# Routing tokens to experts by scattered token numbers, the gate as a column of the row, and logits by pairs of chunks

## The chip, the cores and the metric

The kernel runs on one core of one Trainium2 chip. The metric is the device time of one execution in microseconds (us). Three executions of the kernel before took 446.55, 448.6 and 443.81 us; their median is 446.55.

## What is computed

The reference is a gated linear attention whose result goes through a mixture of experts. Four batches, eight heads, 768 steps, head size 48; `x` is then 3072 tokens by 384.

```
state = alpha[:, :, t, :, None] * state + k[:, :, t] outer v[:, :, t]
y[:, :, t] = q[:, :, t] @ state
x = y.transpose(0, 2, 1, 3).reshape(3072, 384)
logits = x @ w_gate + modality_bias[modality_id]          # 8 experts
e_idx = argmax(logits)
gate = exp(0) / (sum(exp(logits - max)) + 1e-9)
out[token] = gate * (relu(x[token] @ w1[e_idx]) @ w2[e_idx])
```

w1[e] is 384 x 1024 and w2[e] 1024 x 384, all float32. Each token goes to one expert, so the tokens of an expert have to be brought together before its two products.

## The kernel before

**Attention.** The 3072 tokens are 24 chunks of 128, six to a batch. A loop over `s` runs the steps of several chunks side by side: loads of q, k, v, alpha on SP, `decay` (two scans on DVE, L238 and L245), `scale` (L261, L264), `scores` (L273 on PE, a copy on ACT L277, and the causal mask L278, an affine select on POOL, twice per chunk), and three steps later `combine`: the state's update (matmuls L305 into the PSUM tile "kv", DVE L308), the output matmuls L318 and L320, and the copy `yt` (L322). From `yt` the chunk's logits are made: L341 multiplies it with the gate weights into "kv", ACT copies that (`lts`), L347 sums the four head pairs by a matmul with `sel8` into "kv" again, and DVE adds the bias (L348). "kv" has one buffer. `rows` transposes yt (L329) and writes 128 rows of x to the DRAM table `xd`.

**Routing.** After chunks 5, 11, 15, 17, 21 and 23 a route group (table GROUPS) takes the logits of the 6, 6, 4, 2, 4 and 2 chunks since the last group: the maximum, the first expert that reaches it (one small DVE operation per chunk, L396), one-hots, the rank of each token among its expert's tokens by matmuls with a triangle (L400 to L406), and then per chunk on DVE the token's own rank (L408), the number of full 128s in it (L418) and a plane `OL`, 128 x 128, that holds the token's number at its rank (L424). Slots of 256 tokens of one expert are the units of the experts' work. The table of which token stands where in a slot is a sum of matmuls of those planes with one-hots of the slots: for slots 0 and 1 early, after chunks 15 and 17 (`route_early`, L508), for all others in `route_end` once chunk 23 is done, where counts of tokens become runs, keys (L549, L553), the schedule `meta` (L554) and 24 matmuls (L566, marked "table"). `places` makes `idx` (for gathers) and `odx` (for the output) of it. The gates are made apart (`gates`), written to DRAM as a column `gd` and gathered by the same indices (`gather_gates`, L611).

**Experts.** Twelve full slots, then conditional ones: at slot i, inside `If(ns > i)`, either a full slot or a half one of 128 tokens. In this run there is one half slot, 12. For each slot SP loads the weights (4 transfers of 768 KB, two sets of buffers), POOL gathers rows (`xg`, L606, two of 128 rows, three buffers) and gates; `prep` transposes the rows on PE (L758); `split` makes high and low parts of weights on ACT and DVE (L767, L769), and the products are three matmuls each (L788 to L790, L809 to L811; half slot L838 and L850 to L852). The output rows are scaled by the gate (L813, half slot L854) and scattered to DRAM on POOL (L815, L856). `prep(i + 1)` is called at the end of slot i.

**What sets the order.** Each engine runs its instructions in the order in which a scheduler put them before the launch; a waiting instruction holds everything behind it on its engine. `issue_after` keeps a few matmuls behind marks: the first layer of slot 0 is cut into steps by the table STEPS, and layer 2 of slot 0 comes after the mark "table".

## Time and profile before

| what | before |
|---|---|
| three executions | 446.55, 448.6, 443.81 us |
| the profiled execution, its span | 449.16 us, 447.4 us |
| mean granted clock of PE | 0.969 |
| busy: PE, PEld, DVE, ACT, POOL | 406.1, 369.5, 280.3, 238.3, 135.6 us |
| last copy of yt (attention done) | 190.0 us |
| schedule of the slots known (`meta`) | 206.7 us |
| one full slot | 17.6 us |
| last output scatter | 429.0 us |

The busy rows say how long each engine ran at all. A window row gives for a stretch of time the busy time of each engine, with the number of instructions, the granted clock and the DMA engines' share. A row of a group ends in the idle time that its engine had ahead of it and in what ended that idle time. PEld is the loading of weights into PE, which runs beside the matmuls. All times of single instructions are from the span's start.

### The profile page before, as it was taken

The numbers are of one execution on the slowest core, as the hardware profiler recorded it, in microseconds if no ns is written. First come the engines' busy times: TensorE is split into PE (matmuls) and PEld (weight loads), VectorE is DVE, ScalarE is ACT, GpSimd is POOL, SyncE is SP. The second block draws the span as 40 slices with busy tenths as digits, with TensorE's granted clock in tenths as the row PEclk, the third lists the DMA queues.
The fourth block names the chain that finished last, engine by engine and source line by source line (L and its number), as shares of the span: only waits on it lengthen the run. The fifth ranks groups of instructions, "written<-read, shape, count | busy, mean of one in ns | idle before, by whom it ended". The sixth has DMA issues, their size and how long they took to land. (4 is left out here: it accounts for less than half of the span.)

```text
span 447.4 us, 10022 instructions
## 1 busy us (share of the span) xinstructions
PE 406.1 (91%) x3784; PEld 369.5 (83%) x3784; DVE 280.3 (63%) x659; ACT 238.3 (53%) x455; POOL 135.6 (30%) x183
## 2 busy tenths in 40 slices
PE   3999998999999899887999999999999999999620
PEld 3878887888788678665999999999999999999620
DVE  7877679687959793476964766575575675430400
ACT  3476766666575544373655757556565565332310
POOL 9321212111121523200727524343353332110500
PEclk9999999999999899996999999999999999999985
DMA  7999776477556766103997785585586765730200
GB/s 148 202 195 207 145 170 134 99 163 170 114 108 145 268 219 237 38 19 95 379 387 236 279 285 165 203 307 192 193 258 214 232 205 170 262 109 20 58 14 1
DMA packets 134685, 78.81 MB, mean 176 GB/s; under 512 B 103905, under 2 KB 121374, under 8 KB 134616
## 3 DMA queue, kind: packets, MB, share of 16 engines
q1 hardware_dynamic: 130328, 67.72, 54.3%
q0 software_dynamic: 4288, 10.24, 6.3%
q8 instruction: 35, 0.57, 0.5%
q14 instruction: 34, 0.28, 0.2%
HBM read 68.49 MB, written 9.65 MB: 175 GB/s over the span
## 5 line engine op out<-in xcount | busy, mean ns | idle before, releaser
L769 DVE TENSOR_TENSOR w2L<-w2r,w2H 128x768 fp32r<-128x768 f32 x52 | 49.3, 956 | 51.8 <-ACT w2H L767 50.5
L788 PE MATMUL tr<-xH,w1H 128*128 128x256 f32 x264 | 75.8, 287 | 2.4 <-DVE hL L794 2.3
L789 PE MATMUL tr<-xL,w1H 128*128 128x256 f32 x264 | 74.8, 283 | 0.0
L790 PE MATMUL tr<-xH,w1L 128*128 128x256 f32 x264 | 74.6, 283 | 0.0
L278 POOL TENSOR_SCALAR_AFFINE_SELECT scT<-scT 128x512 f32<-128x512 f32 x48 | 30.8, 664 | 121.5 <-ACT scT L277 121.5
L809 PE MATMUL sc<-w2H,hH 128*128 128x384 f32 x192 | 64.4, 337 | 0.0
L810 PE MATMUL sc<-w2L,hH 128*128 128x384 f32 x192 | 64.0, 335 | 0.0
L811 PE MATMUL sc<-w2H,hL 128*128 128x384 f32 x192 | 62.6, 335 | 0.0
L767 ACT CAST w2H<-w2r 128x768 fp32r<-128x768 f32 x52 | 42.7, 833 | 35.4 <-PE sc L811 30.7
L815 POOL DMA_INDIRECT out_dram<-os,odx x24 | 25.9, 1078 | 103.0 <-ACT os L813 70.7
L769 DVE TENSOR_TENSOR w1L<-w1r,w1H 128x768 fp32r<-128x768 f32 x44 | 41.8, 957 | 22.2 <-ACT w1H L767 17.7
L788 PEld LDWEIGHTS tr<-xH,w1H 128*128 128x128 f32 x264 | 50.6, 192 | 3.0 <-DVE hL L794 2.5
L767 ACT CAST w1H<-w1r 128x768 fp32r<-128x768 f32 x44 | 36.3, 834 | 31.0 <-PE tr L789 18.5
L789 PEld LDWEIGHTS tr<-xL,w1H 128*128 128x128 f32 x264 | 50.7, 192 | 0.0
L790 PEld LDWEIGHTS tr<-xH,w1L 128*128 128x128 f32 x264 | 50.4, 191 | 0.0
L606 POOL DMA_INDIRECT xg<-xd,idx x28 | 35.0, 1251 | 43.8 <-DVE vals L475 29.4
L320 PE MATMUL y<-scT,vt 128*64 128x128 f32 x384 | 44.4, 279 | 0.0
L318 PE MATMUL y<-qh,UB 128*64 128x128 f32 x320 | 41.0, 282 | 0.4 <-ACT UB L299 0.4
L794 DVE SCALAR_TENSOR_TENSOR hL<-tr,hH 128x512 fp32r<-128x512 f32 x48 | 32.9, 685 | 13.0 <-ACT hH L792 13.0
L611 POOL DMA_INDIRECT gg<-gd,idx x28 | 31.9, 1138 | 18.9 <-DMA gd<-gs 9.1
L792 ACT ACTIVATE hH<-tr 128x512 fp32r<-128x512 f32 x48 | 28.5, 593 | 16.1 <-PE tr L790 8.7
L809 PEld LDWEIGHTS sc<-w2H,hH 128*128 128x128 f32 x192 | 36.3, 189 | 0.0
(220 smaller groups left out, 810.8 us busy)
## 6 DMA issues: line engine op xcount, KB each, us to landing
w1r<-in_moe_w_dram SPq DMA_DIRECT2D x28, 768.0 KB
w2r<-in_moe_w_dram SPq DMA_DIRECT2D x28, 768.0 KB
nat_a<-in_alpha_dram SPq DMA_DIRECT2D x24, 192.0 KB
nat_k<-in_k_dram SPq DMA_DIRECT2D x24, 192.0 KB
nat_q<-in_q_dram SPq DMA_DIRECT2D x24, 192.0 KB
vt<-in_v_dram SPq DMA_DIRECT2D x24, 192.0 KB
xd<-xs SPq DMA_DIRECT2D x24, 192.0 KB
xg<-xd,idx POOLq DMA_INDIRECT x28, 6.6
```

What stands on the lines that cost most here:

```text
L318: pe.matmul(y[r, j], U[:, j, g], qh[:, j], start=True, stop=False)
L320: pe.matmul(y[r, j], vt[:, 2 * j + g], sc[g][:, j], start=(c == 0), stop=True)
L606: pool.indirect_dma_start(xg[i % NX][:, u], None, xd[0:rows], ix, bounds_check=rows - 1, oob_is_err=False)
L767: act.copy(hi, src)
L769: vec.tensor_tensor(lw, src, hi.bitcast(F32), op=ALU.subtract)
L788: pe.matmul(hp[:, z], wH[:, d, fs], xH[:, d], start=(d == 0), stop=False)
L789: pe.matmul(hp[:, z], wH[:, d, fs], xL[:, d], start=False, stop=False)
L790: pe.matmul(hp[:, z], wL[:, d, fs], xH[:, d], start=False, stop=(d == ND - 1))
L794: vec.scalar_tensor_tensor(hL, hp, 0.0, hH.bitcast(F32), op0=ALU.max, op1=ALU.subtract)
L809: pe.matmul(op, hH[:, z, us], wH[:, z], start=(f == 0), stop=False)
L810: pe.matmul(op, hH[:, z, us], wL[:, z], start=False, stop=False)
L811: pe.matmul(op, hL[:, z, us], wH[:, z], start=False, stop=(f == NF - 1))
```

## The change

The table of places is not summed by matmuls any more but written by scatters. Each expert has 3072 places in a DRAM table `tab`, filled with an empty mark at the start. A route group computes for each token its place, expert base plus rank, as one number `dst` (the base is carried in the running counts `ohs`, which start at 24 x 128 x e), and POOL scatters the chunk's 128 token numbers there, one transfer per chunk (L425, 24 in all). A slot is a run of 256 places: SP loads the place at which it begins (`begin`, L544), then the 256 numbers (`ids`, L545), and POOL gathers the rows by them (L548); the output scatter uses the same `ids`. The planes OL, the one-hots OH, `places` and the marks "key0" and "table" go; layer 2 of slot 0 stands behind the mark "key".

The small operations of a route group are done for all its chunks at once (L397 to L422), the exponentials for the gate among them. The gate becomes column 384 of the row: `xs` holds the rows of a whole group and goes out in one write after the group's reciprocal (L431, 6 writes, before 24), and a gather brings row and gate together. `gates`, `gd` and `gather_gates` go.

Logits are made for two chunks at a time: L341 has 256 columns, two transposes (L346) take the place of two L347, and one DVE reduction (L347 of the new kernel) sums the four head pairs; the bias is added by group.

In the conditional slots `prep(i)` stands at the start of slot i's own `If` instead of at the end of slot i - 1, so that prep(13) is run only where a slot 13 exists.

The core of the diff:

```diff
-STEPS = (("key", 21), ("key0", 20), ("count", 9), ("rank", 8), ("logits", 6), ("logitst", 4))
+STEPS = (("key", 18), ("count", 9), ("rank", 8), ("logits", 6), ("logitst", 4))
...
-    xd = dr.tile([N + 1, DM], F32, name="xd")
-    gd = dr.tile([N + 1, 1], F32, name="gd")
+    xd = dr.tile([N, W], F32, name="xd")
+
+    tab = dr.tile([E * N, 1], I32, name="tab")
...
-    xg = [cp.tile([P, 2, DM], F32, name=f"xg{i}") for i in range(NX)]
-    gg = [cp.tile([P, 2], F32, name=f"gg{i}") for i in range(NX)]
+    xg = [cp.tile([P, 2, W], F32, name=f"xg{i}") for i in range(NX)]
+
+    NI = 4
+    ids = [cp.tile([P, 2], I32, name=f"ids{i}") for i in range(NI)]
...
+    pool.iota(ti, [[P, NU]], base=0, channel_multiplier=1)
+    none = ac.tile([P, E * NU], I32, name="none")
+    pool.memset(none, EMPTY)
+    sp.dma_start(tab.rearrange("(p x) o -> p (x o)", p=P), none)
+    for t in xg:
+        pool.memset(t, 0.0)
...
-        yt = sb.tile([P, NP, P], F32, name="yt")
-        mark["yt"] = act.copy(yt, y)
-        st[i, "y"] = yt
-
-    def rows(i):
+        yt = sb.tile([P, 2, NP, P], F32, name="yt") if i % 2 == 0 else st[i - 1, "yt"]
+        mark["yt"] = act.copy(yt[:, i % 2], y)
+        st[i, "yt"], st[i, "y"] = yt, yt[:, i % 2]
...
-        sp.dma_start(xd[row(i) : row(i) + P, :], xs)
...
     def logits(i, after=None):
 
-        lt = ps.tile([P, P], F32, name="kv")
+        lt = ps.tile([P, 2, P], F32, name="kv")
         with issue_after(after):
             for j in range(NP):
                 mark["logitst"] = pe.matmul(
-                    lt[32 * j : 32 * j + 32], wgp[:, j], st[i, "y"][:, j], start=True, stop=True
+                    lt[32 * j : 32 * j + 32], wgp[:, j], st[i, "yt"][:, :, j], start=True, stop=True
                 )
-        ls = sb.tile([P, P], F32, name="lts")
+        ls = sb.tile([P, 2, P], F32, name="lts")
         mark["xc"] = act.copy(ls, lt)
-        lp = ps.tile([P, E], F32, name="kv")
-        mark["logits"] = pe.matmul(lp, ls, sel8, start=True, stop=True)
-        vec.tensor_tensor(L[:, i], lp, bt[:, i], op=ALU.add)
+        lp = ps.tile([P, 2, P], F32, name="kv")
+        for c in range(2):
+            mark["logits"] = pe.transpose(lp[:, c], ls[:, c], ident)
+        vec.tensor_reduce(
+            L[:, i - 1 : i + 1], lp.rearrange("p c (j e) -> p c e j", e=32)[:, :, :E], axis=AX.X, op=ALU.add
+        )
...
+        vec.tensor_tensor(L[:, s], L[:, s], bt[:, s], op=ALU.add)
         vec.tensor_reduce(mx[:, s], L[:, s], axis=AX.X, op=ALU.max)
-        for t in range(t0, t1):
-            vec.scalar_tensor_tensor(eq[:, t], L[:, t], mx[:, t : t + 1], rev, op0=ALU.is_equal, op1=ALU.mult)
+        vec.tensor_tensor(ls[:, s], L[:, s], wide(mx), op=ALU.subtract)
+        act.activation(ex[:, s], ls[:, s], AF.Exp)
+        vec.scalar_tensor_tensor(
+            eq[:, s], ls[:, s], 0.0, rev.unsqueeze(1).broadcast_to(sh), op0=ALU.is_equal, op1=ALU.mult
+        )
         vec.tensor_reduce(m2[:, s], eq[:, s], axis=AX.X, op=ALU.max)
-        vec.tensor_tensor(oh[:, s], eq[:, s], m2[:, s].unsqueeze(2).broadcast_to(sh), op=ALU.is_equal)
+        vec.tensor_tensor(oh[:, s], eq[:, s], wide(m2), op=ALU.is_equal)
...
-        for t in range(t0, t1):
-            vec.scalar_tensor_tensor(
-                rj, rp[:, t - t0], 1.0, oh[:, t], op0=ALU.mult, op1=ALU.mult, accum_out=r1[:, t : t + 1]
-            )
...
+        vec.tensor_reduce(sm[:, s], ex[:, s], axis=AX.X, op=ALU.add)
+        vec.tensor_scalar(sm[:, s], sm[:, s], 1e-9, None, op0=ALU.add)
+        vec.reciprocal(xs[:, :n, DM], sm[:, s])
+        vec.tensor_tensor(rk[:, s], rp, oh[:, s], op=ALU.mult)
+        with nc.allow_low_precision("whole numbers"):
+            vec.tensor_reduce(dst[:, s], rk[:, s], axis=AX.X, op=ALU.add)
...
         for t in range(t0, t1):
-            vec.scalar_tensor_tensor(
-                hj, thr, r1[:, t : t + 1], onh, op0=ALU.is_le, op1=ALU.mult, accum_out=hr[:, t : t + 1]
+            d = pool.indirect_dma_start(
+                tab, IOA(dst[:, t : t + 1], 0), ti[:, t : t + 1], None, bounds_check=E * N - 1, oob_is_err=False
             )
-        vec.scalar_tensor_tensor(hi[:, s], m2[:, s], -float(NU), hr[:, s], op0=ALU.mult, op1=ALU.add)
-        vec.scalar_tensor_tensor(lo[:, s], hr[:, s], -float(P), r1[:, s], op0=ALU.mult, op1=ALU.add)
-        for t in range(t0, t1):
-            vec.tensor_scalar(OL[:, t], ioh, lo[:, t : t + 1], tok[:, t : t + 1], op0=ALU.is_equal, op1=ALU.mult)
...
+        sp.dma_start(xd[t0 * P : t1 * P].rearrange("(t p) w -> p t w", p=P), xs[:, :n])
...
-        vec.tensor_scalar(key0, iof[:, :2], off, None, op0=ALU.add)
-        vec.tensor_tensor(
-            OHE[:, :n],
-            key0.unsqueeze(1).broadcast_to([P, n, 2]),
-            hi[:, :n].unsqueeze(2).broadcast_to([P, n, 2]),
-            op=ALU.is_equal,
-        )
-        tp = ps.tile([P, 2], F32, name="rt")
-        for t in range(n):
-            pe.matmul(tp, OL[:, t], OHE[:, t], start=(t == 0), stop=(t == n - 1))
-        places(tp, slice(2 * s, 2 * s + 2))
+            vec.tensor_scalar(off, base, -float(N), None, op0=ALU.mult)
+        vec.tensor_scalar(begin[:, s : s + 1], off[0:1], float(E * N), None, op0=ALU.add)
...
-        kp = ps.tile([P, 2, NH], F32, name="rt")
-        mark["key0"] = pe.matmul(kp[:, 0, :nh], ones[:nh], diag[:nh, 0, :nh], start=True, stop=True)
-        vec.tensor_copy(key[:, :nh], kp[:, 0, :nh])
-        vec.scalar_tensor_tensor(rg, beg[:, :NG], sz, dE, op0=ALU.is_le, op1=ALU.mult, accum_out=kc[:, 1:2])
-        vec.tensor_scalar(diag[:, 1], ident[:, :NH], kc[:, 1:2], None, op0=ALU.mult)
-        mark["key"] = pe.matmul(kp[:, 1, :nh], ones[:nh], diag[:nh, 1, :nh], start=True, stop=True)
-        vec.tensor_copy(meta[:, na:NS], kp[0:1, 1, 0:nh:2])
-        tp = ps.tile([P, nh], F32, name="rt")
-        for g in range(3):
-            n = NU // 3
-            z = slice(g * n, (g + 1) * n)
-            vec.tensor_tensor(
-                OH[:, z, :nh],
-                key[:, :nh].unsqueeze(1).broadcast_to([P, n, nh]),
-                hi[:, z].unsqueeze(2).broadcast_to([P, n, nh]),
-                op=ALU.is_equal,
...
+        vec.tensor_tensor(rg, dC, rm.unsqueeze(1).broadcast_to([P, 2, NG]), op=ALU.mult)
+        vec.tensor_reduce(kc, rg, axis=AX.X, op=ALU.add)
+        kp = ps.tile([1, 2, ns], F32, name="rt")
+        for u in range(2):
+            mark["key"] = pe.matmul(kp[:, u], kc[:ns, u : u + 1], ident[:ns, :ns], start=True, stop=True)
+        vec.tensor_copy(meta[:, na:NS], kp[:, 1])
+        vec.tensor_tensor(begin[:, na:], ior[:, :ns], kp[:, 0], op=ALU.add)
...
             )
-            for t in range(g * n, (g + 1) * n):
-                mark["table"] = pe.matmul(tp, OL[:, t], OH[:, t, :nh], start=(t == 0), stop=(t == NU - 1))
...
-    def gates(t0, t1):
-        z = slice(t0, t1)
-        sh = [P, t1 - t0, E]
-        vec.tensor_tensor(ls[:, z], L[:, z], mx[:, z].unsqueeze(2).broadcast_to(sh), op=ALU.subtract)
...
-    def gather(i, rows=N + 1):
+    def gather(i, rows=N):
+        r = sp.value_load(begin[0:1, i : i + 1], min_val=0, max_val=E * N - T)
+        sp.dma_start(ids[i % NI], tab[bass.ds(r, T)].rearrange("(u p) o -> p (u o)", p=P))
         for u in range(2):
-            ix = IOA(idx[:, 2 * i + u : 2 * i + u + 1], 0)
+            ix = IOA(ids[i % NI][:, u : u + 1], 0)
             pool.indirect_dma_start(xg[i % NX][:, u], None, xd[0:rows], ix, bounds_check=rows - 1, oob_is_err=False)
-
-    def gather_gates(i, rows=N + 1):
...
+            for _, t0, t1 in GROUPS:
+                if t0 <= s - 3 < t1:
+                    if t0 == s - 3:
+                        xsg = sb.tile([P, max(b - a for _, a, b in GROUPS), W], F32, name="xs")
+                    rows(s - 3, xsg[:, s - 3 - t0])
+            if (s - 3) % 2:
+                logits(s - 3, ("step", ND - 1) if s - 3 == NU - 1 else None)
             for after, t0, t1 in GROUPS:
                 if after == s - 3:
-                    route_group(t0, t1)
+                    route_group(t0, t1, xsg)
                     if t1 in EARLY:
                         e = EARLY.index(t1)
                         route_early(e)
                         weights(e, e)
-                        gather(e, row(t1))
-                        if e == NA - 1:
-                            gates(0, t1)
-                            for e in range(NA):
-                                gather_gates(e, row(t1))
+                        gather(e, t1 * P)
...
-            g = gg[i % NX]
+            g = xg[i % NX][:, :, DM]
...
-                with issue_after("table" if ahead and i == 0 else None):
+                with issue_after("key" if ahead and i == 0 else None):
...
-                ix = IOA(odx[:, 2 * i + u : 2 * i + u + 1], 0)
+                ix = IOA(ids[i % NI][:, u : u + 1], 0)
...
                 with tc.If(ns > i):
+                    if i > NS0:
+                        prep(i)
                     with tc.If(nfl > i) as full:
                         ahead_of(i + 1)
                         act.copy(XH[i % 2], xf)
                         vec.tensor_tensor(XL[i % 2], xf, XH[i % 2].bitcast(F32), op=ALU.subtract)
                         slot(i)
-                        if i + 1 < NS:
-                            prep(i + 1)
                     with full.Else():
                         ahead_of(i + 1)
                         half(i)
-                        if i + 1 < NS:
-                            prep(i + 1)
                     tail(i + 1)
```

**The order on POOL.** These rows are POOL's program from the first chunks to the first slots: the affine selects of the scores (two per chunk), gathers of rows (`xg`), of gates (`gg`), and with the change scatters of token numbers (`tab<-ti,dst`). Before:

```order
L278 AFFINE_SELECT scT<-scT 128x512 x40
L606 DMA xg_116<-xd,idx 128x384 x2
L278 AFFINE_SELECT scT<-scT 128x512 x4
L606 DMA xg_117<-xd,idx 128x384 x2
L278 AFFINE_SELECT scT<-scT 128x512 x2
L611 DMA gg_119<-gd,idx 128x1 x2
L611 DMA gg_120<-gd,idx 128x1 x2
L278 AFFINE_SELECT scT<-scT 128x512 x2
L606 DMA xg_118<-xd,idx 128x384 x2
```

The same stretch of the changed kernel:

```order
L277 AFFINE_SELECT scT<-scT 128x512 x18
L425 DMA tab<-ti,dst 24576x1 x6
L277 AFFINE_SELECT scT<-scT 128x512 x12
L425 DMA tab<-ti,dst 24576x1 x6
L277 AFFINE_SELECT scT<-scT 128x512 x8
L425 DMA tab<-ti,dst 24576x1 x4
L277 AFFINE_SELECT scT<-scT 128x512 x4
L548 DMA xg_116<-xd,ids_119 128x385 x2
L425 DMA tab<-ti,dst 24576x1 x2
L277 AFFINE_SELECT scT<-scT 128x512 x3
L548 DMA xg_117<-xd,ids_120 128x385 x2
```

The first six scatters stand between the selects of chunk 8 and those of chunk 9; the gathers of gates are gone.

**The order on DVE at the transition**, behind the last route group: `hL` are the low parts of slot 0's hidden layer, of which there are four, `w1L`, `w2L` the splits of weights, `kc` and `meta` the end of the schedule. Before:

```order
L794 SCALAR_TENSOR_TENSOR hL<-tr,hH 128x512
L547 SCALAR_TENSOR_TENSOR diag<-ident,kc,dz 128x38
L551 SCALAR_TENSOR_TENSOR rg,kc<-beg,sz,dE 128x16
L552 TENSOR_SCALAR diag<-ident,kc 128x38
L550 CAST key<-rt 128x34
L559 TENSOR_TENSOR OH<-key,hi 128x8x34 x3
L554 CAST meta<-rt 1x17
L794 SCALAR_TENSOR_TENSOR hL<-tr,hH 128x512
```

With the change:

```order
L723 SCALAR_TENSOR_TENSOR hL<-tr,hH 128x512
L520 TENSOR_REDUCE kc<-rg 128x2
L698 TENSOR_TENSOR w2L<-w2r_113,w2H 128x768
L723 SCALAR_TENSOR_TENSOR hL<-tr,hH 128x512
L524 CAST meta<-rt 1x17
L525 TENSOR_TENSOR begin<-ior,rt 1x17
L698 TENSOR_TENSOR w2L<-w2r_113,w2H 128x768 x3
L690 TENSOR_TENSOR xL_2860<-kv,xH_2858 128x512
L690 TENSOR_TENSOR xL_2860<-y,xH_2858 128x256
L698 TENSOR_TENSOR w1L<-w1r_114,w1H 128x768 x4
L698 TENSOR_TENSOR w2L<-w2r_115,w2H 128x768 x2
L723 SCALAR_TENSOR_TENSOR hL<-tr,hH 128x512 x2
```

Before, the fourth hL of slot 0 follows `meta` at once; now its third and fourth stand behind nine splits and two xL.

**The order on PE in the half slot 12.** Before:

```order
L838 MATMUL tr<-xf,w1r_112 128x128 x24
L758 MATMUL kv<-ident,xg_117 128x128
L758 MATMUL y<-ident,xg_117 128x128
L850 MATMUL sc<-w2H,hH 128x384
L851 MATMUL sc<-w2L,hH 128x384
L852 MATMUL sc<-w2H,hL 128x384
```

With the change (L766 was L838, L778 to L780 were L850 to L852):

```order
L766 MATMUL tr<-xf,w1r_112 128x128 x24
L778 MATMUL sc<-w2H,hH 128x384
L779 MATMUL sc<-w2L,hH 128x384
L780 MATMUL sc<-w2H,hL 128x384
```

The transposes of slot 13's rows no longer stand between the half slot's first and second layer.

228 lines of the change are left out of this document (79 added, 149 removed).

## The prediction

> **What bounds the kernel now.** I read the page's busy rows first (PE 91%, DVE 63%), then the windows, because those shares mix three stages: attention and routing up to the last chunk (190 us), twelve experts' slots, and one half slot at the end.
>
> ```profile
> core 0: us, PE busy (x) PEld busy (x) DVE busy (x) ACT busy (x) POOL busy (x), PEclk, DMA share, GB/s
> 60.00:70.00 10.00, 10.00 (x124) 8.15 (x122) 9.09 (x25) 7.14 (x18) 2.27 (x4) 1.00 0.83 180
> 70.00:80.00 10.00, 8.85 (x111) 7.17 (x112) 9.42 (x45) 5.07 (x12) 1.22 (x2) 1.00 0.46 100
> 140.00:150.00 10.00, 10.00 (x135) 8.01 (x135) 9.86 (x49) 5.21 (x12) 1.34 (x3) 1.00 0.51 117
> 190.00:200.00 10.00, 7.91 (x52) 6.45 (x53) 6.68 (x27) 7.43 (x13) 0.00 (x0) 1.00 0.06 21
> 200.00:210.00 10.00, 7.64 (x45) 5.26 (x44) 5.87 (x26) 4.11 (x7) 0.00 (x0) 0.72 0.09 18
> 210.00:220.00 10.00, 10.00 (x65) 10.00 (x62) 9.70 (x20) 5.61 (x10) 7.22 (x6) 0.94 1.04 370
> 410.00:420.00 10.00, 7.84 (x63) 7.65 (x61) 4.76 (x6) 4.75 (x7) 4.82 (x4) 1.00 0.14 50
> 420.00:430.00 10.00, 6.59 (x30) 6.25 (x30) 0.00 (x0) 1.33 (x3) 3.20 (x4) 0.83 0.19 41
> 430.00:447.00 17.00, 0.00 (x0) 0.00 (x0) 0.00 (x0) 0.00 (x0) 0.00 (x0) 0.59 0.03 7
> ```
>
> PE sets the pace: full at 60:70 although PEld, the weight loads, has gaps, and full from 210 on. It is not full in three places: where DVE does a route group (70:80, with 45 DVE instructions instead of 25), at the transition (190:210, where 4.4 us of PE are lost and the clock falls to 0.72), and in the tail. So the attention stage answers to PE work and to DVE's bursts; the slots from 210 to 410 answer to PE alone and the change removes no PE work there.
>
> **The attention stage, to 190 us.** The weight-load rows in the window 14:196 show what each PE line costs and waits:
>
> ```profile
> L329 PEld LDWEIGHTS tr<-ident,yt 128*128 128x128 f32 x96 | 10.2, 142 | 2.7 <-ACT yt L322 1.0 <-issue 0.6
> L347 PEld LDWEIGHTS kv<-sel,lts 128*128 128x128 f32 x48 | 7.3, 189 | 3.5 <-issue 3.1 <-ACT X L236 0.2 <-ACT junk L249 0.2
> L341 PEld LDWEIGHTS kv<-yt,wgp 128*32 128x32 f32 x192 | 3.8, 109 | 7.8 <-issue 4.2 <-DVE S L308 2.6 <-DVE S L310 0.3
> L508 PEld LDWEIGHTS <-OL 128*128 128x128 f16 x34 | 1.1, 96 | 0.2 <-issue 0.2
> ```
>
> (a) L347, two passes for each of 24 chunks, becomes two transposes per pair of chunks, 24 in all. A transpose of this shape is what L329 does, 10.2 / 96 = 0.106 us each, so 24 x 0.106 = 2.6 in place of 7.3: -4.7. The early tables' 34 loads (L508) go: -1.3. L341 has half the instructions with twice the columns; the columns are what it streams, so I take 0. Together -6.0 of PE work.
>
> (b) Both lines write the one buffer "kv", which the recurrence's L305 uses too; PE idles 7.8 us before L341 and 3.5 before L347. There are 12 such chains instead of 24. If the waits halve, that is 11.3 / 2 = 5.6; part will turn into the next wait in line, since the pair's chain is as long as a single one's. I take half of it, -2.8, between 0 and -5.6.
>
> (c) DVE. The rows of the same window:
>
> ```profile
> L424 DVE TENSOR_SCALAR OL<-ioh,lo,tok 128x128 f16<-128x128 f16 x22 | 6.8, 373 | 0.2
> L308 DVE TENSOR_TENSOR S<-t,kv 128x192 f32<-128x192 f32 x16 | 5.6, 352 | 18.5 <-PE kv L305 14.3 <-PE sc L118 4.2
> L418 DVE SCALAR_TENSOR_TENSOR hj<-thr,r,onh 128x23 f32<-128x23 f32 x22 | 5.3, 240 | 0.1
> L396 DVE SCALAR_TENSOR_TENSOR eq<-L,mx,rev 128x8 f32<-128x8 f32 x24 | 3.8, 220 | 0.1
> L408 DVE SCALAR_TENSOR_TENSOR rj<-rt,oh 128x8 f32<-128x8 f32 x23 | 3.7, 161 | 3.6 <-PE rt L406 3.6
> L348 DVE TENSOR_TENSOR L<-kv,bt 128x8 f32<-128x8 f32 x24 | 3.5, 148 | 8.1 <-PE kv L347 8.1
> L397 DVE TENSOR_REDUCE m<-eq 128x6 f32<-128x48 f32 (+2 forms) x6 | 1.1, 180 | 0.1
> ```
>
> L424, L418, L396, L408 and L348, one each per chunk, go: 6.8 + 5.3 + 3.8 + 3.7 + 3.5 = 23.1 us. In come eight operations for each of six groups (the bias, the difference from the maximum, the tie rule, the sum of the exponentials, its epsilon, the reciprocal, the product with the ranks, the destination), 48 at the 0.18 of L397, whose 128x48 is the same width: 8.6. The 12 reductions of a pair's logits make 2.2 at that price. Net -12 us of DVE. On the path this counts only where DVE holds PE, as at 70:80 (1.15 us of PE lost); of about three such dips I take 1.2 in all, bounds 0 and -3.
>
> (d) What is added. Each route group ends in scatters on POOL, one per chunk of 128 token numbers. POOL also does the affine selects that the next chunks' scores pass through, and these now stand behind the scatters, which wait for DVE's `dst`.
>
> ```profile
> L606 POOL DMA_INDIRECT xg<-xd,idx x28: 997/1030/2275, 149.9 to 419.2; - x28
> DMA to landing us min/median/max: 4.3/6.6/8.0
> 152.47 1.00 POOL L606 DMA_INDIRECT xg<-xd,idx  x1 [0.30 <-issue]
> 72.97 1.22 POOL L278 TENSOR_SCALAR_AFFINE_SELECT scT<-scT 128x512 f32<-128x512 f32 x2 [4.00 <-ACT scT L277]
> 71.86 0.16 DVE L408 SCALAR_TENSOR_TENSOR rj<-rt,oh 128x8 f32<-128x8 f32 x1
> 84.75 0.32 PE L320 MATMUL y<-scT,vt 128*64 128x128 f32 x1
> ```
>
> The old rank work of the first group is done at 71.9, where its sixth L408 stands (L408 is the product of ranks and one-hots that L417 takes over); I put `dst` there too, at 72. Six scatters at 1.03 + 0.30 take 8.0 us to 80.0, chunk 9's select then ends at 81.2 instead of 74.2, and PE asks for it at 84.75: 3.5 us to spare, so I cost it at 0. At the 2.275 of the slowest row, seen while DVE was 98.6% busy (140:150), six take 15.5, the select ends at 88.7 and PE waits 3.9 us in each group of six. The 1.03 is the median of 28, so I take it and keep the other end. The Trainium skill (SBUF — State Buffer, "SBUF: two separate sides") speaks against this part: descriptors of DMAs issued on GpSimd starve while DVE holds the port that they share, and it tells of 620 ns becoming 3,100. By its 3.1 us six scatters would last 20.4 us and PE would wait 8.9 us per group of six, some 20 us in all; the trace's one row of 2.275 in the DVE-full window agrees in direction, the other 27 do not show it.
>
> (e) What else moves, at nothing. The rows of x go out in 6 writes instead of 24 with the gate as their last column, and the three writes of gates and the 28 gathers of gates go; SP and POOL are idle most of this stage (2.27 of 10 us at 60:70 for POOL), and if that cover failed it would be the selects of (d) that came late. The row write now waits for the whole group and its reciprocal, and nothing reads those rows before a gather. SP takes the ids of slots 0 and 1 behind their weights and stands there until the scatters have landed; every load of chunks that the rest of attention needs is ahead of that in its queue, so what waits behind it is the last row writes. In place of two exponentials come six on ACT, 53% busy.
>
> The sum for the stage: -6.0 - 2.8 - 1.2 = **-10**; bounds -3 (half the PE work turns out hidden, nothing else counts) and -15 (6.0 + 5.6 + 3).
>
> **The transition.** t is the copy of the last chunk's y, 190.0.
>
> ```profile
> L322 ACT COPY yt<-y x24: 563/585/592, 18.1 to 190.0; 128x512 f32<-128x512 f32 x24
> L769 DVE TENSOR_TENSOR w2L<-w2r,w2H 128x768 fp32r<-128x768 f32 x52 | 49.3, 956 | 51.8 <-ACT w2H L767 50.5
> 204.45 0.58 PE L788 MATMUL tr<-xH,w1H 128*128 128x256 f32 x1 [2.27 <-DVE hL L794]
> 206.72 0.16 DVE L554 CAST meta<-rt 1x17 int32<-1x17 f32 x1
> 209.32 0.89 PE L566 MATMUL rt<-OH,OL 128*128 128x34 f16 x24
> 225.10 0.60 PE L758 MATMUL kv<-ident,xg 128*128 128x128 f32 x4
> ```
>
> Gone are the one-hot planes, the 24 matmuls of the table at t+19 and the places behind it; the schedule `meta` comes out near t+12 instead of t+16.7 (my estimate: L418, L424, L547 to L552 with their round trip to PE, and L559 leave the chain ahead of it), and the weights of slot 2 start that much earlier. But DVE then has nine splits, at the 956 ns of L769, and two xL ahead of the last two hL of slot 0, some 9.6 us, which layer 2 of slot 0 needs: from t+12 to t+22. PE runs out of other work at about t+16 and waits for the rest; before, it waited in smaller pieces, and layer 2 began behind the table at t+20, with its hL there. Earlier by the table's work, later by DVE's order: I take **-0.5**, within 3 either way (the PE time lost in 190:210 is 4.4 us, so more than that is not to be had without the clock). A new chain starts here: scatters, then slot 2's ids behind 3.1 MB of weights on SP (8.2 us at the 370 GB/s of 210:220, plus a landing), then its gather. I get ids at t+23 and the rows at no later than t+33; PE wants them at t+35 (225.10 before): 2 us to spare, cost 0, up to +5 if it slips.
>
> **The steady slots.** Per slot two gathers of gates go from POOL and a load of ids comes to SP, in front of the row gather:
>
> ```profile
> 260.65 10.46 SPq L584 DMA_DIRECT2D w2r<-in_moe_w_dram  x2
> 295.53 0.60 PE L758 MATMUL kv<-ident,xg 128*128 128x128 f32 x4
> ```
>
> The ids of slot 6 are issued behind the second half of its w2, at 271.1. With a landing L, two gathers (2.7 us) and 8.0 for their landing the rows are there at 281.8 + L; PE wants them at 295.53. So L may be 13.7; no row of an indirect landing is over 8.0. Cost 0, covered by 17.6 us of matmuls per slot.
>
> **The tail.** Slot 12 is a half slot and slot 13 is empty, yet its prep runs inside slot 12's branch:
>
> ```profile
> 416.11 1.73 PE L838 MATMUL tr<-xf,w1r 128*128 128x128 f32 x14
> 421.66 0.30 PE L758 MATMUL kv<-ident,xg 128*128 128x128 f32 x1 [3.82 <-DMA xg<-xd,idx]
> 427.70 0.34 PE L852 MATMUL sc<-w2H,hL 128*128 128x384 f32 x1
> 428.12 0.58 ACT L854 ACTIVATE os<-sc,gg 128x384 f32<-128x384 f32 x1 [9.60 <-PE sc L852]
> 428.98 1.02 POOL L856 DMA_INDIRECT out_dram<-os,odx x1 [6.19 <-ACT os L854]
> ```
>
> With prep(13) under `ns > 13`, L850 to L852 follow L838 at once: 417.84 plus 24 x 0.174 (their spacing at the full clock) = 422.0 against 428.04. That is **-6.0**; the granted clock of 0.83 in 420:430 should not fall either, which the 0.174 already contains. Bounds -4.5 and -7. From the last scatter to the end of the span (428.98 to 447.4) stays.
>
> **Sum:** -10 - 0.5 - 6 = -16.5. The profiled execution took 449.16 us (span 447.4), 2.6 above the median 446.55; taken off that median, it makes 430.
>
> **Rivals.**
> - *Attention keeps its length* (0.22): a new wait takes each one's place, or DVE's scans set the pace (9.86 of 10 in 140:150). For it: PE is full at 60:70 while loads idle. Against it: DVE itself idles 18.5 us before L308, for PE. Only the tail counts: 446.55 - 6.5 = 440.
> - *Attention gains all of its bound and more* (0.12): -15 there, 425 or less.
> - *Scatters hold the selects* (0.08), at 2.275 us: 3.9 x 2 groups = +8, 438. By the Trainium skill's 3.1 us it would be about 450.
> - *The gather of slot 2 is late* (0.05): +5, 435.
> - *Slower* (0.05): the load of ids lands late in every slot, since 256 numbers of four bytes queue among megabytes of weights. It decides from L = 13.7. At L = 17, 3.3 us for each of nine slots is +30: 460. Against it: nothing on the chip here lands after 8.0.
> - The forecast, with every part at its chosen value, holds 0.48.
>
> **Range and chances.** Time 430. Its own bounds give 422 to 437; to leave out no more than two in ten it reaches to the case of an unchanged attention: 423 to 441. About 1% (4.5 us) is what a measurement of this kernel can tell from no change. Faster by more than that (under 442): 0.86, all cases but the slow one and the upper part of the first rival; within 1%: 0.08; slower: 0.06.
>
> **What would show it.** The 24th copy of yt at about 180 instead of 190 (a); PE full where six-chunk groups are done (c); POOL's scatters at about 1.0 us and no PE wait on a select (d); `meta` 12 us after the last yt; no wait of L758 on `xg` in the slots; no L758 among the half slot's matmuls and 5 to 6 us between L838's end and its output. Wrong it would be if the last yt stayed at 188 or later, or if POOL's rows show scatters over 1.9 us, or if PE waits for `xg`.

## The result: 14% slower, and where 64 us of span went

The changed kernel took **511.26 us** (median) against 445.18 us for the kernel before on the same chip: a ratio of **1.137, 95% interval [1.118, 1.156]**. 430 was predicted. The ratio compares fast executions with fast ones, for the changed kernel two of its four (509.68 and 503.06 us). The profiled execution took 512.84 us with a span of 511.1.

The span is 63.7 us longer, and the rows that start its stages split that up:

| stage (profiled executions) | before | after | difference |
|---|---|---|---|
| attention, to the start of the 24th copy of yt | 190.0 | 254.7 | +64.7 |
| from there to slot 1's first output copy | 45.4 | 50.4 | +4.9 |
| from there to the last full slot's last output copy | 177.1 | 177.9 | +0.8 |
| from there to the half slot's output copy | 15.6 | 9.6 | -6.0 |
| rest of the span | 19.3 | 18.6 | -0.7 |

The tail did what was predicted and the slots stood nearly still; the attention lost almost everything. The starts of the 24 copies of yt, chunks counted from 0, say where. Up to chunk 6 each step is within 2 us of what it was before (5.1 us in sum, 67.0 against 61.9); then chunk 6 to 7 takes 15.9 (9.3 before) and 7 to 8 takes 21.4 (8.6). The same pair returns at chunks 12 to 14 (15.6 and 21.4 against 9.2 and 8.5), and 20 to 22 take 12.5 and 17.0 against 6.7 and 7.4. The windows of the changed kernel (its columns are those of the windows of before):

```profile
core 0: us, PE busy (x) PEld busy (x) DVE busy (x) ACT busy (x) POOL busy (x), PEclk, DMA share, GB/s
60.00:70.00 10.00, 9.26 (x96) 7.07 (x98) 6.43 (x13) 4.54 (x10) 1.22 (x2) 1.00 0.67 120
80.00:90.00 10.00, 8.78 (x98) 6.95 (x96) 4.13 (x7) 3.00 (x6) 7.03 (x7) 0.91 0.75 49
90.00:100.00 10.00, 1.48 (x28) 1.11 (x24) 1.12 (x3) 0.00 (x0) 0.00 (x0) 0.77 0.51 32
160.00:170.00 10.00, 0.78 (x4) 0.79 (x5) 0.00 (x0) 2.15 (x5) 0.28 (x1) 0.50 0.64 70
```

From 90 to 100 hardly any engine works: PE 1.48 of 10 us, ACT and POOL nothing. The DMA engines are half busy and move 32 GB/s; at 60:70 they moved 120 at a share of 0.67. A high share with few bytes means that packets took long. What ended the wait stands in ACT's timeline, and the rows of the DMA view, first for 60:78 and then for 78:106 us, show the loads (the last column is the median time to landing):

```profile
103.19 0.61 ACT L248 ACTIVATE junk<-nat_a,bhi 128x384 f32<-128x384 uint32 x1 [17.21 <-DMA nat_a<-in_alpha_dram]
```

```profile
nat_q<-in_q_dram SPq DMA_DIRECT2D x3, 192.0 KB, 4.3
nat_a<-in_alpha_dram SPq DMA_DIRECT2D x2, 192.0 KB, 3.1
```

```profile
nat_a<-in_alpha_dram SPq DMA_DIRECT2D x1, 192.0 KB, 17.7
nat_k<-in_k_dram SPq DMA_DIRECT2D x1, 192.0 KB, 18.0
nat_q<-in_q_dram SPq DMA_DIRECT2D x1, 192.0 KB, 17.1
tab<-ti,dst POOLq DMA_INDIRECT x6, 18.0
```

A load of q or alpha that landed in 3 to 4 us takes 17 to 18 while the six scatters are under way (k: 18.0, against 5.6), and it goes through SP's queue, not POOL's. Not every packet got slower: of the 7,168 packets of 192 bytes in 78:106 the median still took 15 ns, but 200 took over 100 ns, up to 4.3 us, and these hold 56% of the packets' time. The scatter instructions themselves were cheap, as the tile's view shows:

```profile
L425 POOL DMA_INDIRECT tab<-ti,dst x24: 971/972/1265, 78.7 to 261.8; - x24
DMA to landing us min/median/max: 2.1/5.9/18.4
```

0.97 us each on POOL, where the prediction took 1.03; but landing takes up to 18.4 us. (The row of landings counts the loads of ids too. Of the scatters the trace has the landing of eight, 7.3 to 18.4 us; among the first six it is one, the 18.0 above.) Six instructions write 768 numbers of four bytes, 3 KB in all, and hold up loads of 192 KB each.

### The profile page after: what moved, and what is told of

It is laid out like the page before. It is cut to its first block, busy times and chain, and to the rows that moved or that the text cites. A ratio compares the mean times of both kernels' runs of the same rounds, so it can differ in the third digit from the quotient of the medians.

```text
span 511.1 us, 9532 instructions
## 1 busy us (share of the span) xinstructions
PE 411.3 (80%) x3601; PEld 372.1 (73%) x3601; DVE 261.7 (51%) x502; ACT 235.1 (46%) x443; POOL 127.0 (25%) x177
## 4 chain that ended last, share of the span: by engine, by line
PE 37%; DMA 10%; issue 3%; POOL 1%; DVE 0%; ACT 0%; DVEq 0%; POOLq 0%; ACTq 0%; SPq 0%
DMA xg<-xd,ids 7%; PE tr L719 5%; PE tr L718 5%; PE tr L717 5%; PE sc L739 5%; PE sc L738 5%; PE sc L740 5%; DMA xd<-xs 3%; PE tr L108 1%; PE kv L687 1%; PE y L319 1%; POOL scT L277 0%; PE y L317 0%; PE y L687 0%; POOL xg L548 0%
## 5 line engine op out<-in xcount | busy, mean ns | idle before, releaser
L277 POOL TENSOR_SCALAR_AFFINE_SELECT scT<-scT 128x512 f32<-128x512 f32 x48 | 33.0, 712 | 132.0 <-ACT scT L276 132.0
L739 PE MATMUL sc<-w2L,hH 128*128 128x384 f32 x192 | 63.7, 334 | 0.0
L548 POOL DMA_INDIRECT xg<-xd,ids x28 | 32.1, 1147 | 116.3 <-DMA ids<-tab 91.6
L260 DVE TENSOR_TENSOR kh<-tr,G 128x512 f32<-128x512 f32 x24 | 16.5, 688 | 84.4 <-PE tr L227 84.3
L319 PE MATMUL y<-scT,vt 128*64 128x128 f32 x384 | 48.2, 307 | 14.1 <-POOL scT L277 13.9
L717 PEld LDWEIGHTS tr<-xH,w1H 128*128 128x128 f32 x264 | 50.4, 191 | 0.0
L744 POOL DMA_INDIRECT out_dram<-os,ids x24 | 25.4, 1057 | 90.4 <-ACT os L742 58.8
L319 PEld LDWEIGHTS y<-scT,vt 128*64 128x64 f32 x384 | 34.5, 155 | 17.7 <-POOL scT L277 15.1
L317 PE MATMUL y<-qh,UB 128*64 128x128 f32 x320 | 45.1, 317 | 0.1
L248 ACT ACTIVATE junk<-nat_a,bhi 128x384 f32<-128x384 uint32 x24 | 14.8, 618 | 60.1 <-DMA nat_a<-in_alpha_dram 60.1
```

Source lines behind the costliest of these rows:

```text
L277: pool.affine_select(s, s, [[0, NP], [1, P]], ALU.is_ge, 0.0, base=0, channel_multiplier=-1)
L317: pe.matmul(y[r, j], U[:, j, g], qh[:, j], start=True, stop=False)
L319: pe.matmul(y[r, j], vt[:, 2 * j + g], sc[g][:, j], start=(c == 0), stop=True)
L717: pe.matmul(hp[:, z], wH[:, d, fs], xH[:, d], start=(d == 0), stop=False)
L739: pe.matmul(op, hH[:, z, us], wL[:, z], start=False, stop=False)
```

## The experiments

Three explanations were open: the writes themselves jam the DMA engines, because many of them fall into the same line of DRAM, neighbouring places of one expert being four bytes apart (A or A1 in the expectations; "line" here means 64 bytes, the distance that was tried, and not a size that a run shows); SP's queue came into another order (B); or POOL's selects stand behind the scatters (C).

**No scatters.** The loop of scatters is gone and the table holds made-up valid numbers, so that the slots gather as many rows, but wrong ones:

```
-        for t in range(t0, t1):
-            d = pool.indirect_dma_start(tab, IOA(dst[:, t : t + 1], 0), ti[:, t : t + 1], None, ...)
...
```

> The changed kernel without its 24 scatters; the table of places is filled at the start with valid token numbers instead, so slots gather the wrong rows and the output is not the reference's. Theory A (the four-byte writes to DRAM jam the DMA engines: in 84:92 they were 0.66 busy and moved 19 GB/s, and ACT waited 17.2 us for one alpha load): the last yt comes near 180 to 190 instead of 254.7 and the time is 428 to 442. Rival B (the row write of a whole group stands in SP's queue ahead of the loads that chunk 8 needs, and the loads are late for that): it keeps that write, so it stays above 495. Rival C (POOL's order: selects behind scatters, and behind the gathers of slots 0 and 1 that wait for ids): the scatters' part goes, some 10 to 20 us, and the time is near 485 to 500.

451.89 us, ratio 1.015 [1.007, 1.023]. The last copy of yt starts at 202.8 instead of 254.7, chunk 7 to 8 takes 6.8 us. So nearly all of the loss needs the scatters. But the time is above the 428 to 442 that theory A gave: 12.8 us of the attention's loss are left without them.

**Whole lines, and four bytes 64 apart.** Two kernels keep all 24 scatters, in their places, and keep any two numbers from falling into the same 64 bytes. One writes each number 16 times, a row of 64 bytes; the other writes four bytes as before, but 16 words apart:

```
+    tab = dr.tile([E * N, 16], I32, name="tab")            # rows: ti repeated 16 times
...
+    tab = dr.tile([E * N * 16, 1], I32, name="tab")        # stride: places times 16
+        vec.scalar_tensor_tensor(rk[:, s], rp, 16.0, oh[:, s], op0=ALU.mult, op1=ALU.mult)
```

> The changed kernel with places of 64 bytes: each token number is written sixteen times into a row of its own, the ids are read from the first word of each row; the table's filling is 1.5 MB instead of 98 KB, in the start-up. Theory A1 (many short writes into the same 64-byte line are what jams): no two tokens share a line and each line is written whole, so the last yt comes near 185 to 195 and the time is 430 to 450. A2 (any 128 scattered writes to DRAM by POOL jam the engines, whatever their size): it stays at 495 to 515. B and C: no change either, 500 to 515.

> As the kernel with rows of 64 bytes, but only four bytes of each line are written. If sharing a line is what costs (A1), it is as fast as that one, 430 to 450. If writing a part of a line costs by itself, it stays at 495 to 515, or is worse. B and C: no change, 500 to 515.

452.23 us, 1.013 [1.006, 1.021], and 451.25 us, 1.012 [1.009, 1.015]: both as fast as no scatters at all, though the table's 1.5 MB of empty entries are now written at the start; both lie just above the 430 to 450 that was expected. The stride kernel issues the same number of writes of the same size; its scatters stand on POOL as late and as long as in the changed kernel, and land at once:

```profile
L427 POOL DMA_INDIRECT tab<-ti,dst x24: 971/972/1265, 79.3 to 213.8; - x24
nat_a<-in_alpha_dram SPq DMA_DIRECT2D x3, 192.0 KB, 3.2
nat_k<-in_k_dram SPq DMA_DIRECT2D x3, 192.0 KB, 3.8
tab<-ti,dst POOLq DMA_INDIRECT x6, 2.6
```

2.6 us instead of 18.0 for those scatters of the six whose landing the traces have (two and one), 3.2 and 3.8 instead of 17.7 and 18.0 for the loads (window 78:106 of both); of 13,705 packets of 192 bytes 51 took over 100 ns, 4% of the packets' time. What costs 12.5% of the time before is neither the number of the writes, nor their size, nor their queue, but that neighbours lie four bytes apart and not 64. The Trainium skill (DMA: Bandwidth & Descriptors, "Specifications") says that a transfer under 512 bytes makes a DMA engine read, modify and write; every write here is under that, and only those to neighbouring places are slow, so by these runs smallness alone is not the price. The Trainium skill says on the same page, of remote DMA ("Back-pressure in remote DMA"), that stalled writes stall the engine's other queues. The loads of SP's queue at 17 to 18 us look like that, for writes to the core's own DRAM; that this is the mechanism no run shows.

**The same writes in the kernel before.** 24 scatters of token numbers to consecutive places of an array that nobody reads, added to the kernel before at the end of each route group, with one small DVE operation more per group:

```
...
+        for t in range(t0, t1):
+            d = pool.indirect_dma_start(td, IOA(dj[:, t : t + 1], 0), tj[:, t : t + 1], None, ...)
```

> The kernel before with one thing added: after each route group POOL scatters the group's token numbers, four bytes each, to a DRAM table that nobody reads, to places that follow one another; the index passes through the group's ranks so that it stands where the change has it (one small DVE operation more per group). Theory A: the attention stage loses what it lost in the change, 40 to 65 us, and the time is 485 to 515. Rivals B and C (orders and waits of the change, on SP and POOL): none of them is in here, and the time is 445 to 455, the selects waiting for six scatters of 1.3 us at most.

490.27 us, 1.099 [1.091, 1.108]: 10% on a kernel in which hardly anything else changed. The last copy of yt goes from 190.0 to 221.1, 31 us and so less than the 40 to 65 expected, and the tile's view has the slow landings again:

```profile
L431 POOL DMA_INDIRECT td<-tj,dj x24: 970/982/1956, 72.4 to 237.5; - x24
DMA to landing us min/median/max: 8.2/10.6/18.0
```

So the jam is shown by taking it away twice with every scatter in its place, and by making it. SP's order and POOL's order fall as its cause.

**Where tiles begin** (D). Without scatters 12.8 us of attention were still missing. In the first 20 us, before any routing, the windows of before and of the kernel without scatters read:

```profile
0.00:20.00 20.00, 12.95 (x88) 10.83 (x89) 14.81 (x35) 7.62 (x15) 12.37 (x57) 1.00 0.89 171
```

```profile
0.00:20.00 20.00, 13.36 (x82) 10.28 (x83) 13.98 (x29) 6.95 (x14) 12.52 (x54) 1.00 1.18 148
```

The share (the packets' times added up, which can come to more than 1) is higher and the bytes are fewer, for the same loads. The 192-byte packets of the first 60 us, counted by their time, in ns: count,

```
before               13: 1085, 15: 48609
after                13: 810, 15: 22890, the rest between 16 and 46
```

Half of the pieces have become slow. The tiles that the loads fill begin at byte 98336 of a partition in the kernel before and at 88448 in the changed one, since other tiles ahead of them came and went. A piece is 192 bytes, every 256 bytes; from a start that lies 384 past a multiple of 512, every second piece crosses such a multiple; from 32 past it none does. 128 bytes of padding ahead of the tiles move the start to a multiple of 512:

```
     xf = cp.tile([P, ND, T], F32, name="xf")
+    cp.tile([P, 32], F32, name="pad")
```

> The kernel without scatters (its output is not the reference's) with one thing added: 128 unused bytes per partition ahead of the tiles that q, k, v and alpha are loaded into. In the changed kernel these tiles begin at byte 384 of a 512-byte block of the partition (88448 for the first), and of the 192-byte pieces, 256 bytes apart, every second one crosses into the next block; before they begin at byte 32 and none does. In the first 60 us half of the pieces took 16 to 46 ns there, nearly all 15 ns before. Theory D (the crossing slows the loads, and the start-up, where the DMA engines are full, pays for it): with the pad they begin at byte 0, nearly all pieces take 15 ns again, the sixth yt comes near 62 instead of 67.8, and the time falls by 4 to 7 us to 445 to 448. Rival (the slower pieces come from other traffic in the new program, or cost nothing): pieces or times stay as they were, 450 to 454.

445.05 us, 0.987 [0.978, 0.995], against 1.015 without the pad; 48,594 packets are back at 15 ns, and

```profile
0.00:20.00 20.00, 13.44 (x110) 10.82 (x111) 16.27 (x35) 8.89 (x18) 14.22 (x56) 0.91 0.87 169
```

The last copy of yt starts at 196.6, 6.3 us earlier, and the span is 5.7 us shorter (441.7 against 447.4, 1.3%), within the 4 to 7 expected. By the ratios it is 2.8%, and their intervals allow 1.2 to 4.5. Two other starts agree on the cause: in the kernel with whole rows the tiles begin 288 past a multiple of 512 and in the kernel before with scatters 320 past, where no piece crosses one, and 44,747 and 48,703 packets took 15 ns. On the size there is a row against it: the kernel with whole rows (no crossing) was no faster than the stride kernel (21,795 at 15 ns), and its last copy of yt came only 0.8 us earlier (205.9 against 206.7). Both write 1.5 MB at the start, so what the crossing costs beside that traffic stays open.

**The pairs, both ways.** What is left, 6.6 us in the last copy of yt, sits in three steps, which lose 14.8 us while others gain: 15.2 us at chunk 6 to 7, 12.6 at 12 to 13, 15.7 at 18 to 19, where the kernel before has 9.3, 9.2 and 10.2. Are the pairs of logits to blame (E), or the place of the groups' operations in the new order (F)? One kernel takes the pairs out of the kernel just measured, another puts them alone into the kernel before:

```
...
-                    lt[32 * j : 32 * j + 32], wgp[:, j], st[i, "yt"][:, :, j], start=True, stop=True
+                    lt[32 * j : 32 * j + 32], wgp[:, j], st[i, "y"][:, j], start=True, stop=True
...
```

> As the padded kernel without scatters (its output is not the reference's either), with the logits made chunk by chunk again as before. Theory E (pairs of logits, which hold back the even chunks and bunch the work where a route group follows, cost the 4 to 6 us that each batch boundary lost: from the copy of yt of chunk 6 to that of 7 it took 15.5 us and 9.3 before): the boundary falls back to 9 to 11 us and the time by 6 to 10 us against the padded kernel. Rival F (the group's own operations and the order around them do it): the boundary stays at 14 to 15.5 and the time within 3 us or above, since 24 logits take more of PE than 12 pairs.

> The kernel before with the pairs of logits alone (the bias is added by group). My prediction's step (a) and (b): attention shorter by 3 to 8 us, 438 to 443. Theory E: slower by 5 to 12 us, 451 to 458, with boundaries of 14 us. Rival F: within 4 us of before, boundaries of 9 to 10.

Without pairs 449.3 us, 1.003 [0.999, 1.006]; the three steps stay (16.0, 12.9, 16.3), and the last copy moves from 196.6 to 200.7. With pairs alone 447.37 us, 0.996 [0.993, 0.9998]; the last copy moves from 190.0 to 187.9. So the pairs don't cause the long steps. In the changed order they help, by about 1.6% (0.987 against 1.003). Alone, in the kernel before, it is 0.4%, only just clear of nothing, and the 2.1 us of the last copy are no proof: the next run shows it move by more than that where nothing in the attention changed.

**The tail alone**, in the kernel before:

```
                 with tc.If(ns > i):
+                    if i > NS0:
+                        prep(i)
                     with tc.If(nfl > i) as full:
...
-                        if i + 1 < NS:
-                            prep(i + 1)
```

> The kernel before with prep of a conditional slot moved to the slot's own start, nothing else. The prediction's term for the tail: 6.0 us less (4.5 to 7), 439 to 441. Rival (the wait for the gather of slot 13 only moves to the end of the kernel): within 1 us of before.

442.0 us, 0.986 [0.981, 0.992], 6.1 us by the ratio: the half slot's output comes 9.6 us behind the last full one, not 15.6. The attention of this kernel is that of the kernel before, and yet its last copy of yt starts at 187.5, not 190.0. So a difference of 2.5 us in one profiled execution's last copy of yt says nothing.

**The state first.** A chunk that begins a sequence copies its state out of PSUM on DVE (L310 before: `S<-kv`), and the next chunk's matmuls wait for that. The rows of DVE at chunk 6, first of before, then of the kernel without scatters and with the pad:

```profile
64.44 1.22 DVE L245 TENSOR_TENSOR_SCAN Fw<-X,DF 128x516 f32<-128x516 f32 x1
65.58 0.33 DVE L310 COPY S<-kv 128x192 f32<-128x192 f32 x1
66.34 1.23 DVE L238 TENSOR_TENSOR_SCAN G<-X,DR 128x516 f32<-128x516 f32 x1
```

```profile
65.93 0.21 DVE L405 SCALAR_TENSOR_TENSOR eq<-ls,rev 128x48 f32<-128x48 f32 x1
66.05 1.23 DVE L241 TENSOR_TENSOR_SCAN G<-X,DR 128x516 f32<-128x516 f32 x1
...
68.58 1.19 DVE L248 TENSOR_TENSOR_SCAN Fw<-X,DF 128x516 f32<-128x516 f32 x1
69.68 0.33 DVE L313 COPY S<-kv 128x192 f32<-128x192 f32 x1
...
80.54 0.69 DVE L264 TENSOR_TENSOR kh<-tr,G 128x512 f32<-128x512 f32 x1 [8.21 <-PE tr L231]
```

In the changed order the copy stands behind the next chunk's two scans, and that holds at chunks 6, 12 and 18; in the kernel with pairs alone it stands, as before, between the two. What follows is in the windows of the kernel with the pad, which has the changed order:

```profile
66.00:70.00 4.00, 2.15 (x33) 1.81 (x28) 4.00 (x13) 2.31 (x6) 1.62 (x2) 1.00 0.57 128
70.00:74.00 4.00, 3.67 (x38) 3.32 (x40) 2.33 (x9) 1.40 (x4) 0.00 (x0) 0.52 1.01 301
74.00:78.00 4.00, 3.04 (x30) 2.64 (x26) 0.00 (x0) 0.87 (x2) 0.22 (x1) 0.62 0.32 65
```

PE is idle for 1.85 of 4 us while DVE is full, then its granted clock is 0.52 and 0.62, and DVE, done with everything, waits 8.2 us for PE. One edit puts the copy ahead of the scans:

```
...
+        with issue_after("S" if i % NC == 4 and i > NC else None):
             vec.tensor_tensor_scan(G[:, 1:][:, ::-1], x[:, 1:][:, ::-1], ...)
...
```

> The kernel without scatters and with the 128-byte pad, and one order on DVE: at the three chunks that begin a sequence (6, 12, 18) the copy of the state out of PSUM comes before the tenth, sixteenth and twenty-second forward scan pair's successor, as in the kernel before, instead of behind it. Like its parent it writes no token numbers; the table holds made-up ones. Theory G: what is left of the attention's loss (steps of 15.3, 12.6 and 15.7 us at chunks 6 to 7, 12 to 13, 18 to 19, where the kernel before has 9.3, 9.2 and 10.2) comes from that place in DVE's queue: PE waits for the state, its granted clock falls to 0.52, and DVE then waits 8.2 us for PE. Then these steps are 9 to 11 us, the last copy of yt starts at 180 to 187 instead of 196.6, and the time is 0.955 to 0.975 of before. Rival H: the steps are long because a group's operations come in one burst, wherever the copy stands; then they stay over 14 us, the last copy stays at 194 to 198 and the time at 0.98 to 0.99 of before.

430.27 us, 0.961 [0.956, 0.966]. The three steps are 9.7 us each and the last copy starts at 182.7. The group's operations stand here in one unbroken burst, so the burst is not the cause; the copy's place in DVE's queue is. The windows at the same chunk:

```profile
66.00:70.00 4.00, 4.00 (x69) 3.52 (x67) 3.86 (x14) 3.14 (x8) 1.76 (x2) 1.00 0.58 133
70.00:74.00 4.00, 3.13 (x50) 2.65 (x48) 3.96 (x11) 2.39 (x6) 0.39 (x1) 1.00 1.01 297
74.00:78.00 4.00, 4.00 (x52) 2.96 (x49) 1.32 (x2) 2.46 (x6) 1.22 (x2) 1.00 0.91 178
```

**The whole kernels.** First the kernel before with pairs and tail; then the changed kernel with everything in it and three mends (places 64 bytes apart with the empty entries written during chunks 3 to 6, the pad, the state first):

```
+        if 3 <= s < 7:
+            sp.dma_start(tab.rearrange("(p a b) o -> p a (b o)", p=P, a=16)[:, 4 * s - 12 : 4 * s - 8], ...)
```

> The kernel before with the pairs of logits and with the last prep moved under its condition, nothing else. If the two gains are independent: 0.9961 x 0.9864 = 0.983 of before, about 437.5 us, last copy of yt at 186 to 188, last half slot's output 9.6 us behind the last full one. Rival: the pairs' 2 us in the attention are given back at the transition, as they seem to be when alone, and it stays at the tail's 0.986.

> The changed kernel, whole, with three mends: places 64 bytes apart, so that no two scattered numbers lie in one line, with the table's 1.5 MB of empty entries written in four pieces while chunks 3 to 6 are loaded; the 128-byte pad; the state copied first. If shared lines, the tiles' start and the state's place are the whole loss: 0.955 to 0.98 of before, last copy of yt at 181 to 190, and it beats the kernel before by its tail and its transition. If the write of the empty entries collides with the loads of chunks: yt of chunks 4 to 8 come 4 to 8 us late and the time is 0.97 to 0.99. If something else in the scatters costs, 1.0 or more.

The first: 441.08 us, 0.986 [0.980, 0.991], last copy of yt at 187.4. That is the tail's gain alone (last copy of yt 187.5 there), and the product of both, 0.983, lies in the interval too: whether the pairs add to it, these runs can't tell. The second: 444.7 us, 0.993 [0.990, 0.997], above the 0.955 to 0.98 expected and slower than its twin without scatters by some 3%. The steps into chunks 7, 13 and 19 are good (10.0, 9.9, 10.4), but 8 to 9 takes 11.5 us and 13 to 14 takes 11.4, against 7.4 and 6.9 in the twin. POOL's rows and the windows there:

```profile
71.80 1.22 POOL L426 DMA_INDIRECT tab<-ti,dst  x1 [3.20 <-DVE S L308]
...
78.43 0.97 POOL L426 DMA_INDIRECT tab<-ti,dst  x1 [0.30 <-issue]
79.40 2.17 POOL L278 TENSOR_SCALAR_AFFINE_SELECT scT<-scT 128x512 f32<-128x512 f32 x2
```

```profile
80.00:84.00 4.00, 2.03 (x27) 1.60 (x28) 3.90 (x8) 1.67 (x4) 1.58 (x2) 0.76 0.51 98
84.00:88.00 4.00, 4.00 (x27) 3.78 (x28) 0.32 (x1) 2.43 (x6) 1.22 (x2) 0.50 0.25 49
```

Behind a block of six scatters PE idles about 2 of 4 us, and then its clock is at half. The last kernel spreads the scatters of the first two groups, two behind each of the next three pairs of selects:

```
+        if s in (10, 11, 12, 16, 17, 18):
+            with issue_after("sel"):
+                scatter(2)
...
```

> The kernel of the run just ahead (places 64 bytes apart, the pad, the state first), with the six scatters of the first and of the second group no longer one behind the other on POOL but two behind each of the next three pairs of selects. Ahead of it, two steps behind each group's scatters lasted 11 us (81.4 to 92.9, and 121.4 to 132.8) where the kernel without scatters has 7.4 and 6.9. Theory C': these steps are long because the selects stand behind six scatters of 1.27 us each; PE then misses 2 us, its granted clock falls to 0.50, and that doubles the loss. Then both steps are under 9 us, the last copy of yt is at 187 to 191 instead of 197.0, and the time 0.970 to 0.985 of before. Rival I: the loss is the 1.5 MB of empty entries and the scatters' writes among the loads (one guard waits 2.7 us for its chunk); then the spread changes nothing, last copy at 195 to 198, time 0.99 to 1.0.

**436.81 us, 0.969 [0.963, 0.975]**. The two steps are 7.9 and 6.9 us, the last copy of yt starts at 186.4, and the windows read

```profile
80.00:84.00 4.00, 3.83 (x61) 3.42 (x58) 1.84 (x5) 3.02 (x7) 1.35 (x3) 1.00 0.58 111
84.00:88.00 4.00, 4.00 (x50) 3.09 (x46) 3.48 (x7) 2.06 (x6) 2.81 (x2) 1.00 0.73 140
```

So in this kernel six scatters in one block cost what two at a time do not: 8.1 us of span (441.8 against 433.7). The theory's numbers came, a little better than said, but not its wait: no row shows PE waiting for a select there. What the rows show is a late release. The four transpositions of nat_k and the DVE operation that takes them, with the block and then spread:

```profile
75.41 0.60 PE L227 MATMUL tr<-ident,nat_k 128*128 128x128 f32 x4
79.05 0.69 DVE L261 TENSOR_TENSOR kh<-tr,G 128x512 f32<-128x512 f32 x1 [5.71 <-PE tr L227]
```

```profile
75.35 0.60 PE L227 MATMUL tr<-ident,nat_k 128*128 128x128 f32 x4
75.99 0.69 DVE L261 TENSOR_TENSOR kh<-tr,G 128x512 f32<-128x512 f32 x1 [2.70 <-PE tr L227]
```

The transpositions end at 76.0 in both; kh starts at 75.99 spread and at 79.05 with the block. It is not DVE alone: the load that takes nat_k's buffer again starts on SP's queue at 76.11 and at 79.04, and ACT's copy of nat_a's transpositions at 75.98 and at 77.60. All of them wait for PE. But a block alone does not do this. In the stride kernel, which has the same blocks of six, the rows inside its second block (129.6 to 136.9) are prompt:

```profile
136.14 0.60 PE L229 MATMUL tr<-ident,nat_k 128*128 128x128 f32 x4
136.78 0.69 DVE L262 TENSOR_TENSOR kh<-tr,G 128x512 f32<-128x512 f32 x1 [7.19 <-PE tr L229]
```

Its steps 8 to 9 and 13 to 14 take 7.7 and 7.0 us. What more it takes for PE's work to count as done 3 us late stays open.

The spread kernel is the whole computation, 3% faster than the kernel before, and its interval lies below that of the kernel before with pairs and tail (0.980 to 0.991).

## Why the prediction was wrong, step by step

**(d) is the step that failed**: "Six scatters at 1.03 + 0.30 take 8.0 us ... so I cost it at 0." Only the instruction's time on POOL was priced, and that was right (a median of 0.97 us). The 128 writes behind each instruction were not priced at all. The row of indirect gathers from which the price came reads whole rows of x, each in lines of its own; the scatter writes single words side by side. The ratio of 1.137 falls to 1.012 when each number has 64 bytes to itself. In the mended kernel the block stands where the step put it: it begins at 71.8 (72 said), the select behind it ends at 81.6 (81.2 said), and PE does not wait for that select. Yet the block costs 8 us of span there, with the late release of kh, which the step did not know; the rival with scatters that hold the selects gave that size (8) for another reason, which is luck. Against the Trainium skill's 3.1 us (SBUF — State Buffer, "SBUF: two separate sides") stand 0.97 to 1.27 us in the changed kernel, with no scatter over 1.97 in any other.

**(c) priced the right work and missed the order.** The groups' operations of that list (48) took 9.7 us where 8.6 were expected, the pairs' reductions 2.4 (2.2):

```profile
L347 DVE TENSOR_REDUCE L<-kv 128x16 f32<-128x64 f32 x12 | 2.4, 198 | 30.0 <-PE kv L346 30.0
L419 DVE TENSOR_REDUCE dst<-rk 128x6 int32<-128x48 f32 (+2 forms) x6 | 1.0, 175 | 0.0
```

DVE has 11 us less to do, and "of about three such dips I take 1.2 in all" became a loss: the new order put the copy of the state behind a pair of scans, which costs 13.9 us of attention (196.6 against 182.7) and by the ratios 2.6% of the time. The order of the rows was there to be read before the run; I looked for how far the group's operations moved, not for what else moved with them.

**(a) and (b) were right in work and too large in effect.** PE's loads:

```profile
L346 PEld LDWEIGHTS kv<-ident,lts 128*128 128x128 f32 x24 | 3.2, 148 | 0.0
L339 PEld LDWEIGHTS kv<-yt,wgp 128*32 128x32 f32 x96 | 1.9, 110 | 2.2 <-issue 2.2
```

L347's 7.3 us became 3.2 (predicted 2.6), and L341's 3.8, which I left as they were, became 1.9. The waits ahead of both went from 11.3 to 2.2 us, more than half. Yet the pairs alone brought the last copy of yt forward by 2.1 us, which is within what it moves by itself (4.1 in the other comparison), and not by 8.8: most of this lay beside other work.

**(e) missed the addresses.** Tiles that were added and removed moved others by 9,888 bytes, which cost 5.7 us of span (1.015 to 0.987 by the ratios). Nothing in the diff touches these loads.

**The transition** was sized at -0.5. It came out at +4.9 in the changed kernel, still within the jam, and at -6.3, -6.7 and -5.9 in the kernels without it (slot 1's first output 39.1, 38.7 and 39.5 us behind the last copy of yt, against 45.4). The term had the right sign and a tenth of its size. `meta` stood 11.4 us behind the last copy of yt in the last kernel (12 said, 16.7 before), so the gain came as estimated and the loss by DVE's order was put too high; that this is all of it is argued, and no run took it apart.

**The slots and the tail were right**: +0.8 us over all the slots where 0 was predicted, and -6.0 in the tail where -6.0 was predicted, in the changed kernel and with the tail alone. The slower rival, ids that land late in every slot, did not happen: the slots keep their 17.6 us.

With the four faults mended the change gives 0.969, which on the median shown at the outset is 433 us, within the predicted range (423 to 441), though by other terms: attention -3.6 instead of -10 (and -1.1 against the trace of the tail alone), transition -5.9 instead of -0.5, tail -6.0. That the total fits is luck. Two sums of the prediction were off without consequence: its parts' bounds add up to 421 and 442, not to 422 and 437, and 3.1 MB at 370 GB/s take 8.4 us, not 8.2.

## What to carry to other kernels

A DMA issue has two prices, the instruction on its queue and what its packets do to everyone's packets: for small scattered writes ask how close together they fall, and give each room of its own; 64 bytes were enough here. A high DMA share with few bytes per second is the sign of slow packets, whoever waits. Before believing a sum of saved work, read the order in which a scheduler now issues what PE waits for, and the start addresses of tiles that the change never names.
